# Sigmoid attention and a mixed-block product: unmixed weight blocks kept at their own scale, adds on GpSimd, and another order of seven products

## The chip, the cores and the metric

The kernel runs on one core of one Trainium2 chip. The metric is the device time of one execution in microseconds (us). The core has five engines that run side by side and wait for one another through semaphores: TensorE (PE in the profile, with its weight loads as PEld), VectorE (DVE), ScalarE (ACT), GpSimd (POOL) and SyncE (SP), which here issues nearly all DMAs.

## The reference

The input is 8 batches of 12 heads of attention over 448 positions of 64 values. Its output, 3584 rows of 768, goes through two matrix products with a bent curve between them.

```python
scores = scale * np.matmul(q, k.transpose(0, 1, 3, 2)) - np.log(S)   # q, k, v: 8 x 12 x 448 x 64
attn = 1.0 / (1.0 + np.exp(-scores))
x = np.matmul(attn, v)                       # brought to 3584 x 768
h = x @ w_in                                 # w_in: 768 x 2048
g = np.where(h >= 1, h, np.where(h <= -1, 0, (h + 1) ** 2 / 4))
out = g @ w_out                              # w_out: 2048 x 768
```

## The kernel before

**Numbers in two halves.** Most operands are split into a high and a low f16 half, with a scale that is a power of two, and a product is made of three f16 matmuls (high by high, high by low, low by high). `w_in_sb` holds 16 chunks of w_in, each as two halves of 768 columns; chunks 0 to 7 have the scale `wi.scale[0]`, chunks 8 to 15 `wi.scale[1]`.

**Stages.** Attention is done in pairs of heads, six for a batch; each pair is cut into pieces whose scores (`scores`, L385 to L403), sigmoid (`weigh`, L432 to L444) and product with v (`av`, L476) follow one another. A pair's data is loaded three pairs ahead and split two pairs ahead (`prep_b`, L351 to L366; for pairs from 17 on GpSimd does the splitting, L356 to L358). Pieces of the next batch's attention are spread between the units of the MLP of the batch before. The MLP has `ups` (x by w_in), `bend` (the curve, L713 to L717) and `downs` (g by w_out, L736, with its scaling L742 or L746). `finish_x` scales and splits x (L499 on ScalarE, L500 on VectorE) ahead of the ups of batches 0 and 1.

**Batches 0 and 1 and the mixes.** Batches 0 and 1 use w_in as it is (`up`, L700). While batch 1 is under way, `mix(i)` makes, for each of the eight pairs of chunks f = i and g = i + 8, a set of seven blocks of 384 columns, and sends it to the DRAM tensor `blocks[i]`. Four blocks are mixed, that is sums and differences of the four half chunks a11, a12 (of f) and a21, a22 (of g): the halves are added up to f32 (L610, `mixa`), combined (L614 to L617), scaled and split again (L623 on ScalarE, L624 on VectorE, `mixs`) and sent (L627). Three blocks are plain: both halves of f and the right half of g, multiplied to the common scale of the set (L633, `mixp`) and sent (L636). `mixed["to"][0]` and `["to"][1]` are the factors from the scales of f and g to the common one. `mixa`, `mixs` and `mixp` take turns in the two buffers of the tag `raww`.

**Batches 2 to 7 in blocks.** From batch 2 on, `up_blocks(b, i, j)` makes the ups of a pair of chunks with seven products of half size in place of eight: product j multiplies block `wt` of the set by a block `xt` of x (made by `finish_blocks`, L519 to L526) and adds it up in quarter q of two PSUM tiles of one bank each: quarters 0 and 1 lie in `hold[i, 0]`, quarters 2 and 3 in `hold[i, 2]`. Each product is nine matmuls of 224 columns (L666). ScalarE copies (L678, L684) and VectorE adds (L675) bring the quarters together in hf and hg, which `bend` takes. A matmul with `start=True` begins the sum anew; the others add to it. The three sets in SBUF lie where w_in was; `load_set` (L642) brings in set n + 2 when product 2 of set n is reached, and must wait until the buffer's former set has been used by its last product.

**What sets the order.** The Tile framework makes each engine's instruction stream when the program is built: it goes by priorities (the order in which the code asks for the work, shifted by `tc.high_priority`) and by a model of when each instruction will be ready, and passes over those that aren't. On the chip each engine then runs its stream in that order. The pool `ps_mo` has three PSUM banks, which the tiles `pm`, `ph` and `po` take in turn.

Of the kernel before, what the change touches and what calls it, by code (L numbers as in the profile page):

```python
# [15 lines left out]
F16 = mybir.dt.float16  # L16
BF16 = mybir.dt.bfloat16
I32 = mybir.dt.int32
AF = mybir.ActivationFunctionType
ALU = mybir.AluOpType  # L20
# [3 lines left out]
P = 128  # L24
# [30 lines left out]
QA = 17  # L55
QT = 3
WOP = 6
MIXP = 0
CORN = 10
TP = 1  # L60

# [11 lines left out]
def sigmoid_attention_mlp(ctx: ExitStack, tc: tile.TileContext, first_qvk, qkv, w_in, w_out, out_t):  # L73
    nc = tc.nc
    NFULL, _, _, S = first_qvk.shape
    B = out_t.shape[1] // S
    NFC, _, DM = w_out.shape
# [10 lines left out]
    raw_p = ctx.enter_context(tc.tile_pool(name="raw", bufs=2))  # L88
# [14 lines left out]
    w_in_sb = const.tile([P, NFC + 1, 2, DM], F16, name="w_in_sb")  # L103
# [7 lines left out]
    HN, NB, HC = S // 2, 7, NCC // 2  # L111
# [8 lines left out]
    blocks = drm_p.tile([NFC // 2, P, SET], F16, name="blocks")  # L120

    def scales(m, n, tag, pool=None, square=False, less=0):
# [24 lines left out]
        out=ident, in_=ident, pattern=[[-1, P]], compare_op=ALU.is_equal, fill=0.0, base=0, channel_multiplier=1  # L147
# [438 lines left out]
    mixed = {}  # L586
# [17 lines left out]
    def mix(i):  # L604

        to, ratio, minus = mixed["to"], mixed["ratio"], mixed["minus"]
        f, g, H = i, i + NFC // 2, DM // 2
        a = raw_p.tile([P, 2 * DM], I32, tag="raww", name="mixa").bitcast(F32).rearrange("p (r n) -> p r n", r=2)
        for r, chunk in ((0, f), (1, g)):
            (nc.gpsimd if r < MIXP else nc.vector).tensor_tensor(  # L610
                out=a[:, r], in0=w_in_sb[:, chunk, 0, :], in1=w_in_sb[:, chunk, 1, :], op=ALU.add
            )
        a11, a12, a21, a22 = a[:, 0, :H], a[:, 0, H:], a[:, 1, :H], a[:, 1, H:]
        nc.vector.tensor_tensor(out=a22, in0=a21, in1=a22, op=ALU.add)  # L614
        nc.vector.scalar_tensor_tensor(out=a21, in0=a11, scalar=ratio, in1=a21, op0=ALU.mult, op1=ALU.subtract)
        nc.vector.scalar_tensor_tensor(out=a11, in0=a11, scalar=minus, in1=a22, op0=ALU.mult, op1=ALU.add)
        nc.vector.scalar_tensor_tensor(out=a12, in0=a12, scalar=ratio, in1=a11, op0=ALU.mult, op1=ALU.subtract)  # L617
        st = raw_p.tile([P, 2 * DM], I32, tag="raww", name="mixs").bitcast(F16)
        sv = st.rearrange("p (r t h n) -> p r t h n", r=2, t=2, h=2)
        for r in range(2):  # L620
            src = a[:, r].rearrange("p (t n) -> p t n", t=2)
            hi = sv[:, r, :, 0, :]
            nc.scalar.activation(hi, src, AF.Copy, scale=to[1])  # L623
            nc.vector.scalar_tensor_tensor(  # L624
                out=sv[:, r, :, 1, :], in0=src, scalar=to[1], in1=hi, op0=ALU.mult, op1=ALU.subtract
            )
        nc.sync.dma_start(out=blocks[i][:, 3 * DM :], in_=st)  # L627
        pl = raw_p.tile([P, 2 * DM], I32, tag="raww", name="mixp").bitcast(F16)[:, : 3 * DM]
        pv = pl.rearrange("p (t h n) -> p h t n", t=3, h=2)
        for t0, n, chunk, k in ((0, 2, f, 0), (2, 1, g, 1)):  # L630
            src = w_in_sb[:, chunk].rearrange("p h (t n) -> p h t n", t=2)[:, :, 2 - n :, :]
            for h in range(2):
                nc.vector.tensor_scalar(  # L633
                    out=pv[:, h, t0 : t0 + n, :], in0=src[:, h], scalar1=to[k], scalar2=None, op0=ALU.mult
                )
        nc.sync.dma_start(out=blocks[i][:, : 3 * DM], in_=pl)  # L636

    def load_set(n):

        if n < (B - SB) * NFC // 2:  # L640
            dst = sets[n % 3].rearrange("p t h n -> p (t h n)")
            nc.sync.dma_start(out=dst, in_=blocks[n % (NFC // 2)])  # L642
# [3 lines left out]
        common_scales(b, small("invq", inv_x, 0.25, ALU.mult), small("ihc", inv_x, mixed["inv"], ALU.mult))  # L646


    PRODUCTS = (0, 0, 0), (3, 4, 1), (5, 5, 2), (6, 3, 3), (1, 1, 0), (2, 6, 2), (4, 2, 3)

    def up_blocks(b, i, j):

        n = (b - SB) * (NFC // 2) + i
        if j % 2 == 0 and j < 4:
            hold[i, j] = ps_mo.tile([P, 512], F32, tag="mo", name="ph")
        if j == 2 and n:
            load_set(n + 2)
        wt, xt, q = PRODUCTS[j]

        def quarter(q):  # L660
            return hold[i, q // 2 * 2][:, q % 2 * 256 : q % 2 * 256 + HN]

        out, w = quarter(q), sets[n % 3]
        for c in range(HC):
            for wh, xh in ((0, 0), (0, 1), (1, 0)):
                nc.tensor.matmul(  # L666
                    out, w[:, wt, wh, c * P : (c + 1) * P], xc[:, xt, c, xh, :],
                    start=j in (0, 2) and c + wh + xh == 0, stop=c == HC - 1 and wh == 1,
                    skip_group_check=True,
                )  # L670

        hf, hg = (rows[:, (i % 2 * 2 + k) * S : (i % 2 * 2 + k + 1) * S] for k in range(2))
        u2, u3 = (rows[:, 4 * S + i % 2 * S + k * HN : 4 * S + i % 2 * S + (k + 1) * HN] for k in range(2))

        add = lambda out, q, other: nc.vector.tensor_tensor(out=out, in0=quarter(q), in1=other, op=ALU.add)  # L675
        with tc.high_priority(offset=Q_PRIO):
            if j == 1:
                nc.scalar.activation(u2, quarter(0), AF.Copy)  # L678
                add(u2, 1, u2)
            elif j == 3:  # L680
                add(u3, 2, u2)
                add(hg[:, HN:], 3, u3)
            elif j == 4:
                nc.scalar.activation(hf[:, :HN], quarter(0), AF.Copy)  # L684
            elif j == 6:
                add(hg[:, :HN], 2, u2)
                add(hf[:, HN:], 3, u2)
        if j == 6:
            bend(b, i + NFC // 2, hg)
            bend(b, i, hf)  # L690
# [16 lines left out]
    def bend(b, f, h):  # L707

        ihr, hr, rt, ihs, _ = up_sc[b, int(f >= NA)]
        g = tmp_p.tile([P, S], F32, tag="tmp", name="g")  # L710
        hi = ghl[:, f, 0, :]

        nc.scalar.activation(g, h, AF.Relu, bias=hr, scale=ihr)  # L713
        nc.vector.scalar_tensor_tensor(out=g, in0=g, scalar=rt, in1=g, op0=ALU.min, op1=ALU.mult)  # L714
        nc.vector.scalar_tensor_tensor(out=g, in0=h, scalar=ihs, in1=g, op0=ALU.mult, op1=ALU.max)  # L715
        nc.scalar.activation(hi, g, AF.Copy)  # L716
        (nc.gpsimd if f % GPOOL else nc.vector).tensor_tensor(out=ghl[:, f, 1, :], in0=g, in1=hi, op=ALU.subtract)  # L717

    part = drm_p.tile([NCC, P, S], F32, name="part")
# [33 lines left out]
    def ups_blocks(b):  # L753

        n = NFC // 2
        order = [(0, j) for j in range(4)]
        for i in range(n):
            if i + 1 < n:
                order += [(i + 1, 0), (i + 1, 1)]
            order += [(i, 4), (i, 5), (i, 6)]  # L760
            if i + 1 < n:
                order += [(i + 1, 2), (i + 1, 3)]
        return [lambda i=i, j=j: up_blocks(b, i, j) for i, j in order]
# [72 lines left out]
    for u, unit in enumerate(units):  # L836
# [3 lines left out]
        if wi.at < NFC + 1:  # L840
            n = NPIECE - WI_A
# [4 lines left out]
        f, r = divmod(u, NCC // 2)  # L846
# [25 lines left out]
    for b in range(1, B):  # L872
# [10 lines left out]
        with ExitStack() as order:  # L883
            if b >= PM:
                order.enter_context(tc.manual_schedule(engines={mybir.EngineType.PE}))
            for u, unit in enumerate(units):
                while at < min(b + 2, B) * NPIECE and (at - first) < share[min(u + 1, last)] * NPIECE:
                    step(at)
                    at += 1
                if b == 1:  # L890
                    while split_at < min(NFC, NA + (u + 1) * (NFC - NA) // (NA * NCC // 2 - 2)):
                        wo.split(split_at, split_at % WOP == 1)
                        split_at += 1
                    while mixed_at < NFC // 2 and u >= MIX0 + mixed_at * (MIX1 - MIX0) // (NFC // 2):
                        mix(mixed_at)
                        mixed_at += 1
                if b + 1 < B and u == last:
                    begun = start_blocks()
                unit()
                if b + 1 < B and u == last:  # L900
                    inv_x = finish_blocks(*begun)
                    block_scales(b + 1, inv_x)
                if b == 1 and u == last - 2:
                    for n in range(3):
                        load_set(n)
# [39 lines left out]
```

## Time and profile before

| | us |
|---|---|
| median of 3 runs | 1183.58 (1179.28 to 1185.38) |
| the profiled execution | 1182.99 |
| its span, first to last instruction | 1181.3 |
| TensorE busy | 1146.3 |
| VectorE busy | 824.9 |
| ScalarE busy | 697.1 |
| GpSimd busy | 321.6 |
| mean granted TensorE clock | 0.987 |

How to read the profile: a row of a group names the line, the engine, the operation, what is written and read, shapes and count; after the bar stand busy us and the mean length of one instruction in ns, and after the second bar the engine's idle time just before them with what ended it. A row of the timeline has start and length in us, and in brackets the engine's idle time before it and what ended it. A row of a stretch has its bounds, its length, then busy us and instructions of PE, PEld, DVE, ACT and POOL, the granted clock, the DMA share and GB/s. Matmuls are pipelined, so the mean length of one is longer than its share of the busy time.

### The profile page before, as it was taken

What the parts mean: (1) busy time and instruction counts of PE and PEld (TensorE: products, weight loads), DVE (VectorE), ACT (ScalarE), POOL (GpSimd) and SP (SyncE); (2) the same over time, 40 slices, a digit from 0 to 9 for tenths busy, and PEclk for the clock granted to TensorE, in tenths of its full rate; (3) what the DMA queues carried; (4) which work ended last, traced back from release to release, by engine and by line L of the source; (5) the groups of instructions that cost most, each with busy time, mean ns of one, the idle gap of its engine ahead of it and who ended that gap; (6) DMA issues with size and microseconds to landing.
All of it is one profiled execution on the core that took longest, in us unless ns stands there. A gap on an engine that the chain in (4) does not pass through costs nothing.

```text
span 1181.3 us, 20203 instructions
## 1 busy us (share of the span) xinstructions
PE 1146.3 (97%) x7662; PEld 669.0 (57%) x7662; DVE 824.9 (70%) x1760; ACT 697.1 (59%) x1158; POOL 321.6 (27%) x389
## 2 busy tenths in 40 slices
PE   5889999899999999999999999999999999999998
PEld 1224433344445776457755677457764677558954
DVE  4877999898945588467973689466883678736830
ACT  5975885665743587447763577546874486513410
POOL 0004310000332254325354236232534253310000
PEclk8899999899999999999999999999999999999999
DMA  9941544447532366224643165424552146302400
GB/s 361 335 150 61 195 149 132 151 142 244 176 109 64 119 213 212 64 64 150 253 146 100 33 251 193 132 64 141 196 207 68 61 155 223 117 25 98 153 16 32
DMA packets 58113, 170.01 MB, mean 144 GB/s; under 512 B 8608, under 2 KB 39840, under 8 KB 51872
## 3 DMA queue, kind: packets, MB, share of 16 engines
q1 hardware_dynamic: 56288, 159.29, 39.4%
q10 hardware_dynamic: 1728, 9.44, 2.3%
q8 instruction: 60, 0.98, 0.3%
q14 instruction: 37, 0.30, 0.1%
HBM read 126.94 MB, written 23.40 MB: 127 GB/s over the span
## 4 chain that ended last, share of the span: by engine, by line
PE 76%; DVE 9%; DMA 8%; ACT 4%; issue 1%; POOL 1%; SPq 0%; ACTq 0%; DVEq 0%
PE po L736 35%; PE ph L666 23%; PE pav L476 8%; PE psc L394 3%; PE psc L403 3%; DMA blocks<-mixs 2%; PE ph L700 2%; DMA w_out_sb<-w_in 2%; PE psc L389 1%; DMA raw<-qkv 1%; ACT a L432 1%; DVE g L714 1%; DMA w_out_sb<-w_out 1%; DMA w_in_sb<-blocks 1%; DVE mixs L624 1%
## 5 line engine op out<-in xcount | busy, mean ns | idle before, releaser
L736 PE MATMUL po<-ghl,w_out_sb 128*128 128x448 f16 x2304 | 445.7, 353 | 0.9 <-DVE g L715 0.9
L736 PEld LDWEIGHTS <-w_out_sb 128*128 128x128 f16 x2304 | 221.8, 98 | 216.6 <-issue 14.0
L666 PE MATMUL ph<-w_in_sb 128*128 128x224 f16 x3024 | 307.7, 259 | 2.0 <-DMA w_in_sb<-blocks 1.6
L666 PEld LDWEIGHTS <-w_in_sb 128*128 128x128 f16 x3024 | 282.6, 98 | 30.9 <-issue 27.4
L444 DVE SCALAR_TENSOR_TENSOR ahl<-psc,ahl 128x896 f16<-128x896 f32 (+1 forms) x170 | 152.9, 900 | 112.7 <-ACT ahl L443 110.4
L435 ACT ACTIVATE psc<-psc,nls,sqk 128x896 f32<-128x896 f32 (+1 forms) x136 | 129.4, 971 | 114.7 <-PE psc L403 97.2
L356 POOL TENSOR_SCALAR raw<-raw,qkv_s 128x448 f32<-128x448 f32 (+1 forms) x93 | 71.3, 781 | 452.9 <-DVE qkv_i L136 363.0
L443 ACT ACTIVATE ahl<-psc 128x896 f16<-128x896 f32 (+1 forms) x170 | 126.9, 762 | 32.9 <-DVE ahl L444 31.8
L700 PE MATMUL ph<-xhl,w_in_sb 128*128 128x448 f16 x576 | 115.5, 358 | 5.2 <-DVE xhl L500 2.9
L675 DVE TENSOR_TENSOR xhl<-ph,xhl 128x224 f32<-128x224 f32 x240 | 87.7, 382 | 26.2 <-PE ph L666 19.7
L322 ACT ACTIVATE dump<-raw 128x448 f16<-128x448 f32 (+1 forms) x105 | 61.8, 588 | 69.0 <-DMA raw<-qkv 68.0
L476 PE MATMUL pav<-ahl,v 128*64 128x448 f16 x748 | 95.6, 359 | 0.0
L713 ACT ACTIVATE g<-xhl,hr,ihr 128x448 f32<-128x448 f32 x96 | 68.7, 752 | 44.0 <-DVE xhl L675 43.1
L716 ACT ACTIVATE ghl<-g 128x448 f16<-128x448 f32 x128 | 72.7, 573 | 36.7 <-DVE g L715 36.3
L700 PEld LDWEIGHTS <-w_in_sb 128*128 128x128 f16 x576 | 55.9, 99 | 64.0 <-issue 16.4
L717 DVE TENSOR_TENSOR ghl<-g,ghl 128x448 f16<-128x448 f32 x128 | 85.6, 675 | 7.1 <-ACT ghl L716 6.6
L714 DVE SCALAR_TENSOR_TENSOR g<-g,rk 128x448 f32<-128x448 f32 x112 | 81.1, 739 | 10.7 <-ACT g L713 10.5
L746 DVE TENSOR_SCALAR o<-po,od 128x448 f32<-128x448 f32 x48 | 32.5, 679 | 65.8 <-PE po L736 65.6
L358 POOL TENSOR_TENSOR hl<-raw,hl 128x448 f16<-128x448 f32 x62 | 70.0, 1149 | 0.0
L394 PE MATMUL psc<-qk 128*128 128x448 f16 x252 | 66.6, 354 | 0.4 <-issue 0.3
L715 DVE SCALAR_TENSOR_TENSOR g<-xhl,ihs,g 128x448 f32<-128x448 f32 x96 | 65.5, 699 | 0.3
L385 PE MATMUL psc<-ghl 64*128 64x448 f32 (+1 forms) x128 | 37.4, 672 | 21.9 <-ACT a L432 17.1
(156 smaller groups left out, 1150.0 us busy)
## 6 DMA issues: line engine op xcount, KB each, us to landing
w_in_sb<-blocks SPq DMA_DIRECT2D x48, 1344.0 KB, 6.5
raw<-qkv SPq DMA_DIRECT2D x34, 704.0 KB, 4.9
qk<-hl SPq DMA_DIRECT2D x320, 56.0 KB, 2.0
w_out_sb<-w_in SPq DMA_DIRECT2D x16, 768.0 KB, 10.9
out_t<-o SPq DMA_DIRECT2D x48, 224.0 KB, 1.9
blocks<-mixs SPq DMA_DIRECT2D x8, 768.0 KB, 4.3
w_out_sb<-w_out ACTq DMA_DIRECT2D x6, 768.0 KB, 4.3
raww<-w_out ACTq DMA_DIRECT2D x6, 768.0 KB, 5.4
```

Source lines behind the costliest of these rows:

```text
L394: nc.tensor.matmul(out, kq[:, j, 1, w], kq[:, j, 0, :], start=True, stop=False)
L435: nc.scalar.activation(a, a, AF.Sigmoid, bias=nls, scale=sqk)
L443: nc.scalar.activation(hi, x, AF.Copy, scale=ATT)
L444: nc.vector.scalar_tensor_tensor(out=lo, in0=x, scalar=ATT, in1=hi, op0=ALU.mult, op1=ALU.subtract)
L476: nc.tensor.matmul(pav[j * D : (j + 1) * D, :S], *terms[j][t], start=c == 0 and t == 0, stop=mid and t == len(terms[j]) - 1,)
L666: nc.tensor.matmul(out, w[:, wt, wh, c * P : (c + 1) * P], xc[:, xt, c, xh, :], start=j in (0, 2) and c + wh + xh == 0, stop=c == HC - 1 a ...
L675: add = lambda out, q, other: nc.vector.tensor_tensor(out=out, in0=quarter(q), in1=other, op=ALU.add)
L700: nc.tensor.matmul(ph[:, :S], w_in_sb[:, f, wh, c * P : (c + 1) * P], xhl[:, c, xh, :], start=c == 0 and wh + xh == 0, stop=c == NCC - 1 a ...
L714: nc.vector.scalar_tensor_tensor(out=g, in0=g, scalar=rt, in1=g, op0=ALU.min, op1=ALU.mult)
L716: nc.scalar.activation(hi, g, AF.Copy)
L717: (nc.gpsimd if f % GPOOL else nc.vector).tensor_tensor(out=ghl[:, f, 1, :], in0=g, in1=hi, op=ALU.subtract)
L736: nc.tensor.matmul(po[:, :S], w_out_sb[:, f, wh, m * P : (m + 1) * P], ghl[:, f, gh, :], start=f == lo and wh + gh == 0, stop=f == hi - 1 ...
```

## The change

In `mix`, the two adds that bring the halves of a chunk together run on GpSimd in place of VectorE. The three plain blocks are no longer scaled into a buffer: three DMAs per pair send them to `blocks[i]` straight from `w_in_sb`, with the scale of their chunk. So the factors come in later, in `up_blocks`: the copies of quarter 0 (j = 1 and j = 4) take the factor of f, and the product with the plain block of g, which is now the last one, begins quarter 2 anew and is multiplied by the factor of g and added to u3 in one instruction. The product of quarter 3 that was last is now the one before it, and its add follows at j = 5.

```diff
     for r, chunk in ((0, f), (1, g)):
-            (nc.gpsimd if r < MIXP else nc.vector).tensor_tensor(
+            nc.gpsimd.tensor_tensor(
                 out=a[:, r], in0=w_in_sb[:, chunk, 0, :], in1=w_in_sb[:, chunk, 1, :], op=ALU.add
             )
...
         nc.sync.dma_start(out=blocks[i][:, 3 * DM :], in_=st)
-        pl = raw_p.tile([P, 2 * DM], I32, tag="raww", name="mixp").bitcast(F16)[:, : 3 * DM]
-        pv = pl.rearrange("p (t h n) -> p h t n", t=3, h=2)
-        for t0, n, chunk, k in ((0, 2, f, 0), (2, 1, g, 1)):
-            src = w_in_sb[:, chunk].rearrange("p h (t n) -> p h t n", t=2)[:, :, 2 - n :, :]
-            for h in range(2):
-                nc.vector.tensor_scalar(
-                    out=pv[:, h, t0 : t0 + n, :], in0=src[:, h], scalar1=to[k], scalar2=None, op0=ALU.mult
-                )
-        nc.sync.dma_start(out=blocks[i][:, : 3 * DM], in_=pl)
+        for t, chunk, part in ((0, f, 0), (1, f, 1), (2, g, 1)):
+            dst = blocks[i][:, t * DM : (t + 1) * DM].rearrange("p (h n) -> p h n", h=2)
+            nc.sync.dma_start(out=dst, in_=w_in_sb[:, chunk, :, part * H : (part + 1) * H])
...
-    PRODUCTS = (0, 0, 0), (3, 4, 1), (5, 5, 2), (6, 3, 3), (1, 1, 0), (2, 6, 2), (4, 2, 3)
+    PRODUCTS = (0, 0, 0), (3, 4, 1), (5, 5, 2), (6, 3, 3), (1, 1, 0), (4, 2, 3), (2, 6, 2)
...
-                    start=j in (0, 2) and c + wh + xh == 0, stop=c == HC - 1 and wh == 1,
+                    start=j in (0, 2, 6) and c + wh + xh == 0, stop=c == HC - 1 and wh == 1,
...
             if j == 1:
-                nc.scalar.activation(u2, quarter(0), AF.Copy)
+                nc.scalar.activation(u2, quarter(0), AF.Copy, scale=mixed["to"][0])
                 add(u2, 1, u2)
             elif j == 3:
                 add(u3, 2, u2)
                 add(hg[:, HN:], 3, u3)
             elif j == 4:
-                nc.scalar.activation(hf[:, :HN], quarter(0), AF.Copy)
+                nc.scalar.activation(hf[:, :HN], quarter(0), AF.Copy, scale=mixed["to"][0])
+            elif j == 5:
+                add(hf[:, HN:], 3, u2)
             elif j == 6:
-                add(hg[:, :HN], 2, u2)
-                add(hf[:, HN:], 3, u2)
+                nc.vector.scalar_tensor_tensor(
+                    out=hg[:, :HN], in0=quarter(2), scalar=mixed["to"][1], in1=u3, op0=ALU.mult, op1=ALU.add
+                )
```

More of the change, by code (lines that the diff above doesn't have):

```diff
@@ L57 @@
 WOP = 6
-MIXP = 0
 CORN = 10
```

## The prediction

> **What bounds the kernel now.** I read the page first (busy shares), then the busy time of each engine by stretch, then the list of who waited for whom on TensorE, then the timeline around each of TensorE's waits.
>
> ```profile
> span 1181.3 us, 20203 instructions
> PE 1146.3 (97%) x7662; PEld 669.0 (57%) x7662; DVE 824.9 (70%) x1760; ACT 697.1 (59%) x1158; POOL 321.6 (27%) x389
> ```
>
> ```profile
> 206.70:236.30 29.60, 26.55 (x120) 10.70 (x119) 25.91 (x61) 19.13 (x26) 1.72 (x1) 0.88 0.43 151
> ...
> 180.00:325.00 145.00, 138.73 (x728) 63.46 (x727) 132.88 (x270) 91.50 (x143) 19.71 (x20) 0.98 0.51 171
> ...
> 413.50:443.00 29.50, 29.50 (x266) 22.42 (x264) 25.18 (x56) 24.37 (x46) 16.37 (x20) 1.00 0.60 213
> ...
> 360.00:1181.30 821.30, 815.29 (x6036) 532.45 (x6033) 534.08 (x1191) 454.07 (x783) 258.35 (x320) 1.00 0.37 127
> ```
>
> Columns of the second fence: stretch, its length, busy PE, PEld, DVE, ACT, POOL, granted clock, DMA share, GB/s. TensorE is the bound: from 360 us on it idles 6 us in 821. The blocks (batches 2 to 7) run there, so making VectorE's work lighter there buys nothing. The one stretch in which VectorE is nearly full (132.88 of 145) and TensorE misses 6.3 us is 180 to 325, batch 1, where the mixes of w_in are made. There the clock also falls, to 0.88 in one slice.
>
> ```profile
> PE psc L385 <- ACT a L432: 17.1, 8, 4.2
> ...
> PE ph L700 <- DVE xhl L500: 2.9, 1, 2.9
> PE ph L700 <- DVE g L715: 1.9, 1, 1.9
> PE ph L666 <- DMA w_in_sb<-blocks: 1.6, 1, 1.6
> PE po L736 <- DVE g L715: 0.9, 1, 0.9
> ...
> PE psc L389 <- DVE ahl L444: 0.4, 1, 0.4
> PE ph L666 <- DVE xhl L675: 0.4, 1, 0.4
> ```
>
> TensorE's waits: total us, times, longest. L385 is the start of the program, which the change leaves alone. In batch 1 stand 2.9, 1.9, 0.9 and 0.4, together 6.1. In the 48 blocks stand 1.6 for a set of weights and 0.4 for an add.
>
> ```profile
> 214.63 0.96 DVE L610 TENSOR_TENSOR mixa<-w_in_sb 128x768 f32<-128x768 f16 x1 [1.72 <-DMA blocks<-mixs]
> ...
> 215.57 1.01 DVE L265 SCALAR_TENSOR_TENSOR w_out_sb<-w_out_sb,wo_s 128x768 f16<-128x768 f32 x1
> 216.50 0.95 DVE L610 TENSOR_TENSOR mixa<-w_in_sb 128x768 f32<-128x768 f16 x1
> 217.37 0.68 DVE L500 SCALAR_TENSOR_TENSOR xhl<-x,x_s,xhl 128x448 f16<-128x448 f32 x1
> ...
> 218.10 6.11 PE L700 MATMUL ph<-xhl,w_in_sb 128*128 128x448 f16 x18 [2.93 <-DVE xhl L500]
> ...
> 256.19 1.83 DVE L610 TENSOR_TENSOR mixa<-w_in_sb 128x768 f32<-128x768 f16 x2 [1.88 <-DMA blocks<-mixs]
> ```
>
> The longest of them is the mix's doing: VectorE stands 1.72 us at L610 for the DMA that must leave the raww buffer, then does both adds, and L500, for which TensorE waits, comes behind. The wait of 0.9 at 260 us follows the same pair, there 1.88 + 1.83 us.
>
> **The change part by part.**
>
> ```profile
> L666 PE MATMUL ph<-w_in_sb 128*128 128x224 f16 x3024 | 307.7, 259 | 2.0 <-DMA w_in_sb<-blocks 1.6 <-DVE xhl L675 0.4
> L444 DVE SCALAR_TENSOR_TENSOR ahl<-psc,ahl 128x896 f16<-128x896 f32 (+1 forms) x170 | 152.9, 900 | 112.7 <-ACT ahl L443 110.4
> L700 PE MATMUL ph<-xhl,w_in_sb 128*128 128x448 f16 x576 | 115.5, 358 | 5.2 <-DVE xhl L500 2.9 <-DVE g L715 1.9
> L675 DVE TENSOR_TENSOR xhl<-ph,xhl 128x224 f32<-128x224 f32 x240 | 87.7, 382 | 26.2 <-PE ph L666 19.7 <-ACT xhl L678 3.4 <-PE psc L156 2.7
> L485 ACT ACTIVATE x<-pav,sqk 128x448 f32<-128x448 f32 x34 | 21.5, 632 | 6.8 <-PE pav L476 6.8
> L610 DVE TENSOR_TENSOR mixa<-w_in_sb 128x768 f32<-128x768 f16 x16 | 14.7, 953 | 6.1 <-DMA blocks<-mixs 6.1
> L262 POOL TENSOR_TENSOR w_in_sb<-w_in_sb 128x768 f16<-128x768 f32 x8 | 14.6, 1829 | 9.2 <-ACT w_in_sb L261 9.2
> L633 DVE TENSOR_SCALAR mixp<-w_in_sb,mixes 128x768 f16<-128x768 f16 (+1 forms) x32 | 9.8, 362 | 0.0
> L482 ACT ACTIVATE x<-pav 128x448 f32<-128x448 f32 x14 | 7.5, 538 | 1.9 <-PE pav L476 1.9
> ```
>
> ```profile
> L627 SPq DMA_DIRECT2D blocks<-mixs x8: 320/330/453, 189.7 to 319.8; - x8
> ```
>
> *Scalings removed.* 32 instructions of L633, 9.8 us of VectorE in batch 1. With them goes the third buffer of each mix: mixa and mixs now alternate on the two raww buffers, so mixa waits for no DMA and L610's 6.1 us of idle go. Late next is mixs, which waits for the DMA of the mixs before it, a whole mix back (130 / 7 = 18 us, by the first and the last issue of L627).
>
> *Adds moved.* 16 adds leave VectorE: 14.7 us. On GpSimd the nearest row is L262, the same 768 elements: 16 x 1.83 = 29.3 us, beside the 19.71 us it is busy in that stretch. L614 and L615 now wait for GpSimd, and whatever is behind them on VectorE with them. GpSimd holds two adds (3.7 us) ahead of whatever it is given next, such as the split of q, k and v late in the stretch; a pair is prepared two pairs ahead, so I count nothing. If that lead were gone, 3.7 us would be the price, once.
>
> ```profile
> 185.43 1.87 POOL L262 TENSOR_TENSOR w_out_sb<-w_out_sb 128x768 f16<-128x768 f32 x1 [19.90 <-ACT w_out_sb L261]
> ...
> 185.71 2.40 DVE L624 SCALAR_TENSOR_TENSOR mixs<-mixa,mixes,mixs 128x768 f16<-128x768 f32 x1
> ...
> 188.64 1.00 DVE L624 SCALAR_TENSOR_TENSOR mixs<-mixa,mixes,mixs 128x768 f16<-128x768 f32 x1
> ```
>
> *What GpSimd's adds take from VectorE.* The same L624 takes 2.40 us under a GpSimd add and 1.00 alone: 1.40 us lost in a collision. So 16 adds cost VectorE between nothing and 22.4 us; I take half, 11, as part of VectorE's work reads PSUM and may not collide. VectorE is relieved of 9.8 + 14.7 + 6.1 - 11 = 20 us in 145.
> The Trainium skill, SBUF — State Buffer, section Who interferes with whom, says that a VectorE instruction with two SBUF inputs contends with a GpSimd instruction that reads SBUF, and that the one that comes later is blocked for the whole instruction; the pair of rows agrees. By that rule, with every add meeting such an instruction, the loss is the upper end, 22.4, and the sum that of rival two.
>
> *Stalls that go.* 2.93 + 0.86 + 1.88 + 0.42 = 6.1 us (the four rows). Behind the first, 18 matmuls of L700 took 6.11 us where 115.5 / 576 = 0.20 each gives 3.6: 2.5 us lost to the lower clock and to L500's pace. At most 8.6 us. I keep one collision, 1.4, in front of an L500, and half of the other three waits, 1.6. Gain 5.6.
>
> *DMAs.* 24 small ones from w_in_sb replace 8 from mixp: 16 more issues on SP.
>
> ```profile
> w_in_sb<-blocks SPq DMA_DIRECT2D x48, 1344.0 KB, 6.5
> ```
>
> 16 x 0.33 = 5.3 us of SP over 130 (L627); each waits only for w_in's split, made long before. The bytes are the same. The sets are read back at 390 us, so nothing waits; if that cover were gone it would be one landing, 6.5.
>
> *Scale in the copies.* L485 (with a scale from SBUF) against L482 (without): 94 ns. On the copies of L678 and L684, 96 in 48 blocks, 9.0 us of ScalarE in 800, of which TensorE sees nothing as long as adds are as early as now. The last add with a scale (scalar_tensor_tensor) costs between an add of 224 (0.38) and L500's 0.68 for 448; I take 0.38: nothing changes.
>
> *The new order.* Now hf's add reads quarter 3 between products 5 and 6, and product 6 writes quarter 2 of the same bank.
>
> ```profile
> 527.62 3.62 PE L666 MATMUL ph<-w_in_sb 128*128 128x224 f16 x36
> ...
> 529.55 0.36 ACT L678 ACTIVATE xhl<-ph 128x224 f32<-128x224 f32 x1 [0.26 <-PE ph L666]
> ```
>
> The first 18 of these matmuls are products 0 and 1 of a block. L678 reads quarter 0, which product 0 had finished at 528.6, yet idle ScalarE starts at 529.55, when product 1 in the other half of the bank has ended. So accesses to one bank are kept apart, and product 6 will wait for that add. Its price by block, if nothing is put between: 0.38 plus some 0.05 to start, 0.43; if an L444 (0.90) is running, 1.28. Between 0 and 48 x 1.28 = 61 us, then; a gain is excluded, for nobody waits on what gets earlier.
> The Trainium skill, PSUM — Partial Sum Buffer, section PSUM bank collisions raise a hardware error, asks for exactly this guard, by bank and not by address; the trace agrees with the 529.55 above. By it the sum would be that of rival one.
> Cover is there: TensorE's order is fixed at build time by a scheduler that passes over what isn't ready. Two products of the next block and the attention's matmuls are free to go in between: 18 matmuls of L666 are 1.83 us (307.7 / 3024 each), more than 1.28.
>
> ```profile
> 547.50 0.69 DVE L675 TENSOR_TENSOR xhl<-ph,xhl 128x224 f32<-128x224 f32 x2 [0.80 <-PE ph L666]
> ...
> 550.08 1.89 PE L666 MATMUL ph<-w_in_sb 128*128 128x224 f16 x18
> ```
>
> As I read the order, these adds free the bank that the 18 matmuls at 550.08 take: ready at 548.2, issued 1.9 us later with other work between. That is the same kind of turn, TensorE to VectorE and back, and over 48 blocks it cost 0.4 us in all. I take 0.02 a block, 1.0.
> *Sum.* The profiled execution took 1182.99 us: 1182.99 - 8.6 + 3.0 + 1.0 = 1178.4. The median of the runs, 1183.58, stands 0.6 above it, so 1179.0.
>
> **The rivals.**
> *One, slower: product 6 waits in the open.* From 0.12 us a block (5.6 / 48) the gain is eaten; at 0.43 it is 20.6 us, less 5.6: 1198.6. For it: VectorE is 85% full where the blocks meet attention (25.18 of 29.5), so an add can come late. Against it: the 0.4 us above.
> *Two, no gain:* GpSimd's adds take back 22.4 us of VectorE's 30.6, mixes wait for GpSimd, and the waits only move: 1183. For it: 185.71. Against it: two of the three long waits have L610 itself in front.
> *Three, everything goes:* all 8.6 us and no price, 1175.0.
> *Four, late sets:* the load of a set starts when product 6 has left its buffer. In batch 7, without attention, one load already cost 1.6 us; product 6 slides up to 1.83 later, and five loads at 1.6 are 8: 1186.
>
> **How the numbers follow.** Half a per cent, 5.9 us, is about what a measurement of this kernel can tell from no change. Forecast (1176 to 1182) 0.50; three 0.13; two 0.19; one 0.13; four 0.05. Faster than 1177.7: three and 0.22 of the forecast, 0.35. Slower than 1189.5: one and 0.04 of two and four, 0.17. The rest, 0.48, is no change. The range goes from just under three to most of one: 1174 to 1194.
>
> **What would show it.** Right: in 180 to 325 VectorE near 119 busy and GpSimd near 49; no wait of L610 for a DMA; the wait of L700 for L500 under 1.5 us and no slice at 0.88; from 360 us on TensorE's idle time as before. Wrong: many waits of L666 for L675 (rival one), L624 and L500 at 2 us (two), more waits for w_in_sb<-blocks after 1073 us (four).

## The result: 0.56% slower

| | before | after |
|---|---|---|
| median of 6 runs each (us) | 1183.84 (1179.28 to 1186.69) | 1189.51 (1188.96 to 1191.48) |
| profiled execution, span (us) | 1182.99, 1181.3 | 1188.96, 1187.2 |

The ratio is 1.0056, with a 95% interval from 1.0037 to 1.0074. I had forecast 1179.0. In the experiments below, one execution of `last_on_gpsimd` took 4055.59 us, against 1178.91 to 1183.07 for its other ten; it is left out of the figures.

### The profile after

Two lines of the page: the span, and each engine's busy time.

```profile
span 1187.2 us, 20204 instructions
...
PE 1143.2 (96%) x7662; PEld 666.3 (56%) x7662; DVE 820.7 (69%) x1712; ACT 704.4 (59%) x1158; POOL 345.9 (29%) x405
```

VectorE and TensorE are busy for less time than before, and yet the program is longer. By stretch (columns as in the prediction), first the kernel before with one batch of blocks, batch 2, from the first matmul of its blocks to the first of the next batch's:

```profile
390.40:527.60 137.20, 137.20 (x1023) 88.48 (x1021) 94.80 (x213) 86.83 (x152) 54.12 (x68) 1.00 0.42 143
```

And the kernel after: batch 1 with the mixes, everything from 360 us on, and the same batch of blocks.

```profile
180.00:325.00 145.00, 138.63 (x749) 64.70 (x748) 124.13 (x233) 92.85 (x150) 49.33 (x42) 0.99 0.45 147
360.00:1187.00 827.00, 813.06 (x6001) 527.56 (x5999) 536.33 (x1184) 458.19 (x776) 251.32 (x318) 1.00 0.37 125
...
384.00:524.00 140.00, 138.01 (x1022) 88.14 (x1021) 95.61 (x213) 87.47 (x152) 53.42 (x68) 1.00 0.42 140
```

A batch of blocks took 137.2 us, all of it TensorE's. It now takes 140.0, of which 2.0 are idle and 0.8 are more time for the same matmuls. From 360 us on TensorE idles 13.9 us, where it had idled 6.0 before; I had named no change there as a sign of being right. In batch 1 VectorE fell from 132.88 to 124.13, but TensorE is no fuller (138.63 for 138.73).

Where the stages begin (their first matmul in the timeline, in us) shows which stages gained and which lost:

| us | before | after | difference |
|---|---|---|---|
| first up of batch 0 | 87.5 | 83.9 | -3.6 |
| last up of batch 0 | 166.8 | 162.1 | -4.7 |
| blocks of batch 2 | 390.4 | 383.9 | -6.5 |
| blocks of batch 7 | 1072.9 | 1079.5 | +6.6 |
| last matmul | 1177.6 | 1183.5 | +5.9 |

So 4.7 us were gained before the mixes had begun, 1.8 in the stretch of the mixes, and 13.1 lost in five batches of blocks (2 to 6). TensorE's waits in those blocks and, in the last three rows, in batch 1 (total us, times, longest):

```profile
PE psc L393 <- DVE ahl L443: 3.3, 9, 1.0
PE ph L659 <- DVE xhl L668: 2.8, 5, 0.6
PE po L732 <- ACT ghl L712: 2.0, 4, 0.7
PE po L732 <- DVE ghl L713: 0.8, 4, 0.2
...
PE ph L696 <- ACT xhl L498: 3.1, 1, 3.1
PE ph L696 <- DVE g L711: 2.3, 2, 1.5
PE ph L696 <- DVE xhl L499: 0.6, 1, 0.6
```

`ahl` are the halves of the attention weights and `ghl` those of g. The first four are new, bar 0.4 for an add and 0.4 for `ahl`, and small one by one: in batch 2 scores wait 0.58 for VectorE's L443, which still reads the PSUM tile that they write, the blocks 0.56 for an add, and the downs 0.85 for ghl, together the 2.0. The last three add up to 6.0, as much as the 6.1 that were to go. The groups of the blocks:

```profile
L659 PE MATMUL ph<-w_in_sb 128*128 128x224 f16 x3024 | 305.0, 259 | 3.5 <-DVE xhl L668 2.8 <-DMA w_in_sb<-blocks 0.7
L668 DVE TENSOR_TENSOR xhl<-ph,xhl 128x224 f32<-128x224 f32 x192 | 72.2, 383 | 23.9 <-PE ph L659 20.1 <-ACT xhl L671 2.9
...
L609 POOL TENSOR_TENSOR mixa<-w_in_sb 128x768 f32<-128x768 f16 x16 | 29.8, 1883 | 48.7 <-DVE qkv_e L129 16.8 <-DVE mixs L623 13.4 <-DVE q L533 11.2
...
L681 DVE SCALAR_TENSOR_TENSOR xhl<-ph,mixes,xhl 128x224 f32<-128x224 f32 x48 | 21.5, 447 | 30.7 <-PE ph L659 30.2
L671 ACT ACTIVATE xhl<-ph,mixes 128x224 f32<-128x224 f32 x48 | 21.3, 444 | 21.9 <-PE ph L659 21.9
```

The scaled copy takes 444 ns, 92 more than before's 352, and the scaled add 447, 65 more than the plain 382.

### The profile page after: what moved, and what is told of

Read it like the earlier page. It is cut to its first block, busy times and chain, and to the rows that moved or that the text cites. A ratio compares the mean times of both kernels' runs of the same rounds, so it can differ in the third digit from the quotient of the medians.

```text
span 1187.2 us, 20204 instructions
## 1 busy us (share of the span) xinstructions
PE 1143.2 (96%) x7662; PEld 666.3 (56%) x7662; DVE 820.7 (69%) x1712; ACT 704.4 (59%) x1158; POOL 345.9 (29%) x405
## 4 chain that ended last, share of the span: by engine, by line
PE 59%; DVE 8%; DMA 3%; POOL 3%; ACT 3%; issue 2%; SPq 1%; POOLq 0%; DVEq 0%
PE po L732 29%; PE ph L659 16%; PE pav L475 5%; PE psc L393 2%; PE ph L696 2%; DMA raw<-qkv 2%; DVE ahl L443 2%; PE psc L402 2%; DVE ghl L713 1%; PE psc L388 1%; DVE g L711 1%; DVE xhl L668 1%; POOL raw L355 1%; DMA w_in_sb<-blocks 1%; ACT dump L321 1%
## 5 line engine op out<-in xcount | busy, mean ns | idle before, releaser
L443 DVE SCALAR_TENSOR_TENSOR ahl<-psc,ahl 128x896 f16<-128x896 f32 (+1 forms) x170 | 152.4, 899 | 77.0 <-ACT ahl L442 74.2
L321 ACT ACTIVATE dump<-raw 128x448 f16<-128x448 f32 (+1 forms) x105 | 61.7, 588 | 87.6 <-DMA raw<-qkv 86.6
L713 DVE TENSOR_TENSOR ghl<-g,ghl 128x448 f16<-128x448 f32 x128 | 92.2, 725 | 19.0 <-ACT ghl L712 18.4
L475 PE MATMUL pav<-ahl,v 128*64 128x448 f16 x748 | 98.8, 360 | 0.7 <-DMA qk<-hl 0.7
L710 DVE SCALAR_TENSOR_TENSOR g<-g,rk 128x448 f32<-128x448 f32 x112 | 81.5, 745 | 21.1 <-ACT g L709 20.1
L668 DVE TENSOR_TENSOR xhl<-ph,xhl 128x224 f32<-128x224 f32 x192 | 72.2, 383 | 23.9 <-PE ph L659 20.1
L711 DVE SCALAR_TENSOR_TENSOR g<-xhl,ihs,g 128x448 f32<-128x448 f32 x96 | 69.4, 739 | 0.3
L475 PEld LDWEIGHTS <-v 128*64 128x64 f16 x748 | 36.4, 109 | 41.3 <-issue 27.6
```

The costliest lines, as they stand in the source:

```text
L443: nc.vector.scalar_tensor_tensor(out=lo, in0=x, scalar=ATT, in1=hi, op0=ALU.mult, op1=ALU.subtract)
L475: nc.tensor.matmul(pav[j * D : (j + 1) * D, :S], *terms[j][t], start=c == 0 and t == 0, stop=mid and t == len(terms[j]) - 1,)
```

## The experiments

My theories after the result: the order of the products costs time in the blocks (A), or the scaled forms do (B), or the mixes and their DMAs do (C). Ratios are against the kernel before, on the same chip.

**Which product waits.** `after_lines` is the changed kernel with its products on lines of their own.

```diff
+                if j == 4: nc.tensor.matmul(*args, **kw)
+                elif j == 5: nc.tensor.matmul(*args, **kw)
+                elif j == 6: nc.tensor.matmul(*args, **kw)
...
```

> The changed kernel with the matmul call of products 4, 5 and 6 written on lines of their own; the instruction streams are those of the changed kernel. Both theories expect 1189 us. Theory one (the bank wait): from 384 us on a batch takes 140.0 us against 137.2 before because the build puts product 6 behind 19 to 35 other matmuls (2 to 6 us) after product 5; the direct wait of product 6 for the add stays under 1 us a batch, and the loss shows as waits of downs for a late bend and of scores for a late attention operation. Theory two (the scaled forms are slower: 447 against 382 ns for the last add, 444 against 352 ns for the copies): the waits stand right behind L681, L671 or L677.

Its one execution took 1189.43 us. The only product with a wait for an add is L664, product 5:

```profile
PE ph L664 <- DVE xhl L675: 2.6, 5, 0.6
...
PE ph L668 <- DMA w_in_sb<-blocks: 0.4, 1, 0.4
```

Product 6, which by rival one would wait for the bank, waits for nothing on the chip. In TensorE's stream, 19 to 35 other matmuls stand between products 5 and 6 of a block in batch 3; in `add_at_6` (below), where no add stands between the two products, there are none in seven of eight blocks. They are products of the next blocks and, in six of the eight blocks, attention's matmuls (behind the last block downs as well). The build hides the bank's wait by putting other work there.

**The order alone, and the order undone.** `order_alone` is the kernel before with the new order of products and plain forms. `add_at_6` is the changed kernel with hf's add after the last product, as before, so that nothing reads the bank between products 5 and 6.

```diff
 order_alone (on the kernel before)
-    PRODUCTS = ..., (1, 1, 0), (2, 6, 2), (4, 2, 3)
+    PRODUCTS = ..., (1, 1, 0), (4, 2, 3), (2, 6, 2)
+            elif j == 5:
+                add(hf[:, HN:], 3, u2)
             elif j == 6:
                 add(hg[:, :HN], 2, u2)
-                add(hf[:, HN:], 3, u2)
 add_at_6 (on the kernel after)
-            elif j == 5:
-                add(hf[:, HN:], 3, u2)
             elif j == 6:
                 nc.vector.scalar_tensor_tensor(...)
+                add(hf[:, HN:], 3, u2)
```

> The kernel before with only the order of the last two products changed and hf's add at j = 5; plain blocks are still scaled in batch 1, nothing is on GpSimd that was not, and quarter 2 goes on adding. Theory one (bank wait): a batch takes 139 to 141 us in place of 137.2, 1192 to 1199 us in all. Theory two (scaled forms): none is here, 1182 to 1186. Theory three (any new order): 1180 to 1195.

> The changed kernel with hf's add moved from j = 5 to j = 6, behind the last product, so that no engine reads the bank between products 5 and 6. Theory one (bank wait): products 5 and 6 stand together again, a batch takes 137.2 to 137.8 us, and the gain of batch 1 (batch 2 starts 6.5 us earlier than before) is left: 1174 to 1179 us. Theory two (scaled forms): they are all still there, a batch still takes 140: 1188 to 1191. Theory three (any new order of instructions moves a batch by some us, up or down): no fixed value, 1176 to 1190.

`order_alone`: 1190.07, ratio 1.0050 (1.0030 to 1.0071). Its first batch of blocks, and its largest wait from 390 us on:

```profile
389.60:528.40 138.80, 138.30 (x1023) 87.80 (x1021) 99.40 (x213) 86.12 (x152) 53.96 (x68) 1.00 0.42 141
```
```profile
PE psc L394 <- DVE ahl L444: 2.9, 5, 1.1
```

The order alone makes a batch 138.8, a little less than the 139 to 141 of my first theory: 0.5 of waits, and 1.1 more for the same matmuls, with no lower clock. What makes them longer is what they stand beside. Where TensorE goes from one of the shapes 128*128, 64*128 and 128*64 to another after a matmul of 448 columns, the next matmul starts 279 to 310 ns after the last (mostly 285), where it is 189 within a run of 448 columns, so some 0.1 us goes at each change. Before has 64 such changes in a batch, `order_alone` 75, the changed kernel 70. Eleven at 0.1 are the 1.1. Over the kernels of this text, in batches without a lower clock, TensorE's busy time goes with the count: 136.2 to 136.5 us with 59 changes, 136.6 to 136.7 with 61, 137.2 to 137.6 with 64, 137.8 with 69, 138.1 with 70 and 138.3 with 75. The Trainium skill, TensorEngine Tiling (Array Packing), section Tiling Modes, says that a change of mode drains TensorE; the starts agree, and put a number to it.

`add_at_6`: 1187.92, ratio 1.0027 (1.0011 to 1.0043). That does not bring the gain back, so A is not the whole. It has only 61 changes, yet its batch takes 140.9. Its largest wait, stretches (one batch, then the time around the turn from ups to downs) and timeline there:

```profile
PE po L738 <- ACT ghl L718: 8.8, 4, 2.5
```
```profile
385.20:526.10 140.90, 138.44 (x1024) 89.00 (x1023) 97.27 (x213) 88.19 (x152) 54.09 (x68) 0.99 0.41 139
...
605.00:612.00 7.00, 4.86 (x27) 2.41 (x26) 1.71 (x4) 5.12 (x11) 0.00 (x0) 1.00 0.50 208
612.00:617.00 5.00, 5.00 (x19) 2.04 (x17) 3.79 (x11) 1.13 (x3) 0.91 (x2) 0.66 0.00 0
```
```profile
606.85 0.58 ACT L321 ACTIVATE dump<-raw 128x448 f16<-128x448 f32 x1 [3.46 <-DMA raw<-qkv]
...
603.24 6.04 PE L738 MATMUL po<-ghl,w_out_sb 128*128 128x448 f16 x31
...
611.41 2.10 PE L738 MATMUL po<-ghl,w_out_sb 128*128 128x448 f16 x7 [2.14 <-ACT ghl L718]
```

In four batches TensorE comes to the last pair's downs before their ghl. ScalarE makes that copy behind L321, which waits for the next pair's raw data. After the 2.14 us the clock is at 0.66 for 5 us, which is another 1.7: together 3.8 in this batch. So it goes in three of the four batches. In the fourth the wait is as long (2.16 us), but the clock stays up behind it, for a reason that no run shows, and the batch takes 138.8:

```profile
892.40:897.40 5.00, 5.00 (x29) 2.23 (x30) 4.00 (x11) 2.62 (x4) 0.34 (x1) 1.00 0.00 0
```

**Is it the scaled forms?** `unscaled_forms` is `add_at_6` with plain copies and a plain last add. `scaled_copies_only` and `scaled_add_only` have one of the two. The factors that are missing in these three are left out of the product, so their outputs are not the reference's; the number of instructions is the same.

```diff
 unscaled_forms (on add_at_6)
-                nc.scalar.activation(u2, quarter(0), AF.Copy, scale=mixed["to"][0])
+                nc.scalar.activation(u2, quarter(0), AF.Copy)
...
-                nc.scalar.activation(hf[:, :HN], quarter(0), AF.Copy, scale=mixed["to"][0])
+                nc.scalar.activation(hf[:, :HN], quarter(0), AF.Copy)
...
-                nc.vector.scalar_tensor_tensor(...)
+                add(hg[:, :HN], 2, u3)
 scaled_copies_only: the last of these three; scaled_add_only: the first two
```

> The kernel of add_at_6 with the two copies of quarter 0 without a scale and the last add as a plain add of u3; the factors of f and g are left out of the blocks, so its output is not the reference's. Theory A: the turn from ups to downs may still be hit; if the dump still comes first, a batch takes 139 to 141 us and the time is 1185 to 1190. Theory B (the 92 ns of each scaled copy and 65 ns of the scaled add, 12 us of ScalarE and VectorE in all, are what makes the chain late): a batch is back at 137.2 and the time is 1172 to 1177.

> add_at_6 with its last add plain: only the two copies of quarter 0 carry the factor of f; the factor of g is left out. Theory one (either scaled form changes the stream that the scheduler builds, and the turn from ups to downs opens again): batches 2 to 6 take 139 to 141 us each as in add_at_6, with a wait of L738's successor for ghl of 1 us or more in batch 3; time 1183 to 1188. Theory two (the copies' 90 ns each are hidden, the add does it): batches near 137.2, time 1175 to 1179.

> add_at_6 with its two copies plain: only the last add carries the factor of g; the factor of f is left out. Theory one (either scaled form changes the stream): batches 2 to 6 take 139 to 141 us, time 1183 to 1188. Theory two (the add, 447 ns for 382 at the end of the block's chain, does it): batches 139 to 141 here, and near 137.2 in scaled_copies_only. Theory three (the copies do it): batches near 137.2 here, time 1175 to 1179, and 139 to 141 in scaled_copies_only.

| | median us | ratio | a batch of blocks, us | changes of shape |
|---|---|---|---|---|
| add_at_6 (both forms scaled) | 1187.92 | 1.0027 (1.0011 to 1.0043) | 140.9 to 138.8 | 61 |
| unscaled_forms | 1176.93 | 0.9965 (0.9953 to 0.9978) | 137.1 to 137.5 | 64 |
| scaled_copies_only | 1175.95 | 0.9936 (0.9913 to 0.9960) | 136.2 to 137.0 | 59 |
| scaled_add_only | 1177.77 | 0.9949 (0.9929 to 0.9969) | 136.6 | 61 |

(Batches 2 to 5.) Without the scaled forms the loss is gone; with either one of them it is gone too. So neither 92 ns on a copy nor 65 ns on an add is the price, and B in its plain form falls, as do the theories that I wrote for the last two. Of these four kernels only the one with both has the bad turn. `scaled_copies_only` at the same place, one batch and the timeline of the turn:

```profile
385.10:521.30 136.20, 136.20 (x1024) 88.51 (x1023) 94.42 (x213) 88.26 (x152) 53.83 (x68) 1.00 0.43 144
```
```profile
598.24 9.48 PE L736 MATMUL po<-ghl,w_out_sb 128*128 128x448 f16 x48
607.56 1.12 PE L393 MATMUL psc<-qk 128*128 128x448 f16 x4
...
610.17 3.01 PE L736 MATMUL po<-ghl,w_out_sb 128*128 128x448 f16 x15
```

Here 48 downs that are ready come in one run, and the next downs come at 610.17 without a wait. In `add_at_6` a run of 31 stands there, and after it TensorE is idle. The matmuls are the same; their order in the stream is another.

**Would another engine close the turn?** In `last_on_gpsimd`, which is `add_at_6` but for this, the high copy for the last pair is made by GpSimd, so that it is not behind L321. `after_last_on_gpsimd` does the same on the changed kernel.

```diff
+        if b >= SB and f % (NFC // 2) == NFC // 2 - 1:
+            nc.gpsimd.tensor_copy(out=hi, in_=g)
+        else:
             nc.scalar.activation(hi, g, AF.Copy)
```

> The kernel of add_at_6, and in batches 2 to 7 the high half of g of the last pair of chunks (7 and 15) is copied by GpSimd in place of ScalarE. Theory A (add_at_6 lost its gain because at the turn from ups to downs the copies of the last pair stand on ScalarE behind a dump that waits for the DMA raw<-qkv): the wait of downs for ScalarE, 2.1 us a batch, and the half clock after it go, a batch takes 137 to 138 us in place of 140.5, and the time is 1173 to 1178. Theory B (the scaled forms make a batch slower wherever they stand): a batch still takes 140, 1186 to 1190.

> The changed kernel, hf's add at j = 5 as it is, with the last pair's high half copied by GpSimd as in last_on_gpsimd. Theory A: the waits of downs for ghl (0.6 to 1.6 us a batch) go, what the order of products costs (1.6 us a batch in order_alone) stays: a batch takes 138.5 to 139.3, 1182 to 1187 us. If the order is the whole loss of the changed kernel, a batch still takes 140 and the time is 1188 to 1190.

```profile
PE po L741 <- DVE ghl L722: 5.9, 4, 2.0
```

`last_on_gpsimd` (the row above): 1180.91, ratio 0.9990 (0.9981 to 1.0000), between my two theories. Four waits at the same place are left, now for the low half on VectorE; only the low clock after them is gone, and a batch takes 138 us. So L321 in front of the copy is a part of it and not all. `after_last_on_gpsimd`: 1186.84, ratio 1.0049 (1.0028 to 1.0071), batches of 139; it has 69 changes of shape, five over before, and 1.46 us of waits in batch 3, and 137.2 + 0.5 + 1.46 is the 139.2 that this batch takes.

**The mixes.** `gpsimd_adds` is the kernel before with the two adds on GpSimd. `last_on_gpsimd_adds_back` is `last_on_gpsimd` with the adds on VectorE.

```diff
 gpsimd_adds
-MIXP = 0
+MIXP = 2
 last_on_gpsimd_adds_back
-            nc.gpsimd.tensor_tensor(
+            nc.vector.tensor_tensor(
```

> The kernel before with only the two adds of each mix on GpSimd; the scaled plain blocks, their buffer and the old order of products stay. If the adds off VectorE bring batch 1's gain, batch 2 starts 3 to 6 us earlier and the time is 1177 to 1181. If collisions on the port of GpSimd and VectorE take it back, batch 2 starts at 390 as before and the time is 1182 to 1186. A batch in blocks takes 137.2 us either way.

> The kernel of last_on_gpsimd with the adds of the mixes back on VectorE. gpsimd_adds started batch 2 no earlier than before (392.3 against 390.4 us). If the adds on GpSimd are a loss by themselves (collisions), batch 2 starts 1 to 3 us earlier than in last_on_gpsimd and the time is 1171 to 1176; if they are part of batch 1's gain, batch 2 starts 2 to 5 us later and the time is 1176 to 1181. A batch in blocks is as in last_on_gpsimd.

`gpsimd_adds`: 1187.19, ratio 1.0025 (1.0011 to 1.0039), above both of my ranges. Its batch 1 and its longest wait there:

```profile
180.00:325.00 145.00, 136.94 (x714) 62.23 (x713) 128.99 (x253) 89.61 (x141) 45.35 (x34) 0.99 0.51 168
```
```profile
PE psc L389 <- POOL v L358: 3.6, 1, 3.6
```

Of the 14.7 us of adds that left VectorE, 12.8 (14 of the 16 adds) had stood in this stretch, and its busy time there fell by 3.9 only: most came back in longer instructions, as in the six L500, 6.5 us for 3.8. And GpSimd's split of v, which follows two of the adds, comes late by 3.6. `last_on_gpsimd_adds_back`: 1181.34, ratio 0.9993 (0.9981 to 1.0006), within the error of `last_on_gpsimd`, though batch 2 starts 3.5 us later in its profile (388.3 for 384.8). The adds on GpSimd earn nothing that the times show.

**A version without the cost.** `scale_in_x` keeps the new mix, and takes the blocks' order, copies and adds from the kernel before. The factors go into x, where `finish_blocks` scales it anyway: blocks 0 and 1 of x meet only f's plain blocks, block 6 only g's. `scale_in_x_vector_adds` has the adds of the mix on VectorE too.

```diff
+        s0, s1 = mixes[:, 6:7], mixes[:, 7:8]
+        for k, o in ((0, s0), (1, s1)):
+            nc.vector.tensor_scalar(out=o, in0=s, scalar1=mixed["to"][k], scalar2=None, op0=ALU.mult)
...
-            nc.scalar.activation(hi, src, AF.Copy, scale=s)
+            st = s0 if t < 2 else s1 if t == 6 else s
+            nc.scalar.activation(hi, src, AF.Copy, scale=st)
...
```

> The mix of the changed kernel (adds on GpSimd, plain blocks sent straight at their own scale), the products' order, plain copies and plain adds of the kernel before; the factors of the plain blocks go into x where finish_blocks splits it, so that blocks 0 and 1 of x carry the factor of f and block 6 that of g, at no instruction per pair of chunks. Theory one (the +2.8 us a batch are the price of the new order and of the scaled forms): batches 2 to 6 return to 137.1 to 137.6 us each, the copies to about 352 ns, the adds to 382; batch 2 starts at 384 to 386 us; the time is 1175 to 1178, ratio 0.993 to 0.997. Theory two (the loss comes from the direct DMAs, from sets that are read back differently): batches stay near 139 to 140 and the time at 1186 to 1190. Theory three (the split of x, now with three factors, puts a new wait between batches): periods 137.2 and one wait of TensorE for xc of 1 us or more at each start of a batch, time 1180 to 1184.

> As scale_in_x, but the two adds of each mix on VectorE as before. Theory one (GpSimd's adds earn what they were meant to in batch 1): batch 2 starts 2 to 4 us later than in scale_in_x and the time is 1178 to 1181. Theory two (the adds on GpSimd are worth nothing, the direct DMAs alone start batch 2 earlier): batch 2 starts within 1 us of scale_in_x, the time within 1.5 us of it. Theory three (GpSimd's adds cost what they take from VectorE, as with the scaled blocks of before): batch 2 starts earlier and the time is 1172 to 1175.

`scale_in_x`: 1179.99 against 1184.89, ratio 0.9955 (0.9939 to 0.9971). `scale_in_x_vector_adds`: 1180.01, ratio 0.9958 (0.9943 to 0.9974). The first is 2 us above my first theory's range. Both are faster than the kernel before, which the changed kernel is not. The batch of blocks of the first, and batch 1 of the second:

```profile
385.10:522.80 137.70, 137.37 (x1023) 88.44 (x1021) 94.43 (x215) 86.75 (x152) 53.78 (x68) 1.00 0.43 143
```
```profile
180.00:325.00 145.00, 138.96 (x744) 64.66 (x742) 127.21 (x248) 93.12 (x149) 23.56 (x27) 0.99 0.45 148
```

A batch takes 137.2 to 138.7 with the direct DMAs in place, so C falls: from 0.9955 to the changed kernel's 1.0056 is 1.0%, 12 us, the size of the 13.1 that the table of starts lays on the blocks. The adds on GpSimd again earn nothing.

## Why the prediction was wrong, step by step

The time fell inside my range, 1174 to 1194, but on the other side of the kernel before, and that it fell inside is partly luck: 4.7 us of gain came from the start, for which I had no reason, and without them the median would be some 1194.

**The new order (forecast 1.0, the step that failed).** I asked what product 6's wait would cost and found that cover would hide it. It did: product 6 never waits. But cover was priced at nothing. What goes in between moves attention's matmuls, of other shapes, to other places: in `order_alone` TensorE changes shape eleven times more in a batch, 1.1 us, and some scores come before VectorE (L444) has read the PSUM tile that they write, 0.5 us. That is 1.6 by five batches, 8 us, and all six batches of blocks of the changed kernel lost 12.4 (13.1, less 0.7 in the last). The chance that I gave to a loss by the order stood on rival one, a wait in the open, which does not occur.

**The scale in the copies (forecast nothing).** Right for each form alone, as the two kernels with one of them show, and wrong for both together: `add_at_6` takes 140.4 to 140.9 in batches 2 to 4 against 136.6 in `scaled_add_only`, with the same 61 changes; 2.14 of wait and 1.7 of clock are 3.8 of the 3.8 to 4.3, and in batch 5, where the clock stayed up, the 2.16 of wait are the whole difference from 136.6 to 138.8. My condition, that TensorE sees nothing as long as adds are as early as now, held for the durations and missed that the build plans with them. The losses by order and by forms do not add up in the changed kernel: its batch is 2.8 longer, 2.0 of it idle.

**Stalls that go (forecast 5.6; TensorE waits as long as before).** The stalls moved, as in rival two, though not at its price: GpSimd's adds took some 11 us from VectorE (below) and not 22.4. The 1.8 that the stretch of the mixes gained are TensorE's busy time, at a granted clock of 0.99 for 0.98; no slice is at 0.88, the lowest at 0.94. At the longest wait, the kernel after (engine's rows, start and length):

```profile
205.25 4.59 POOL L609 TENSOR_TENSOR mixa<-w_in_sb 128x768 f32<-128x768 f16 x2 [1.14 <-DVE mixs L623]
...
209.87 0.56 DVE L613 TENSOR_TENSOR mixa<-mixa 128x384 f32<-128x384 f32 x1 [1.47 <-POOL mixa L609]
...
212.17 0.94 ACT L622 ACTIVATE mixs<-mixa,mixes 128x768 f16<-128x768 f32 x1 [2.37 <-DMA blocks<-mixs]
213.01 3.45 ACT L498 ACTIVATE xhl<-x,x_s 128x448 f16<-128x448 f32 x6
...
213.71 0.73 PE L696 MATMUL ph<-xhl,w_in_sb 128*128 128x448 f16 x3 [3.12 <-ACT xhl L498]
```

L609 waits for no DMA any more, as I had said; I had named mixs as late next and given it 18 us of lead. Two mixes here stand 10 us apart (their L622 at 202.32 and 212.17), and the DMA in between left at 205.13. So ScalarE now waits 2.37 for the buffer, with x's split behind it, where VectorE had waited 1.72. The other two waits are collisions:

```profile
225.04 1.99 DVE L613 TENSOR_TENSOR mixa<-mixa 128x384 f32<-128x384 f32 x1
...
231.12 10.48 PE L696 MATMUL ph<-xhl,w_in_sb 128*128 128x448 f16 x54 [1.53 <-DVE g L711]
...
238.10 2.06 DVE L710 SCALAR_TENSOR_TENSOR g<-g,rk 128x448 f32<-128x448 f32 x1
240.08 1.59 DVE L131 TENSOR_SCALAR qkv_s<-qkv_e 128x3 int32<-128x3 int32 x1
...
242.38 2.81 PE L696 MATMUL ph<-xhl,w_in_sb 128*128 128x448 f16 x14 [0.78 <-DVE g L711]
```

GpSimd does its adds from 221.06 to 225.01, the split of w_out (L261) right behind them to 226.62, and the next two adds from 237.71 to 241.65. L613, L710 and L131 take 0.55, 0.67 and 0.15 elsewhere. L613 meets L261, the other two meet the adds, and VectorE goes from them without a pause to the L711 that TensorE waits for.

**What came out as forecast.** GpSimd's adds: 29.8 us for 29.3. What they take from VectorE: I took 11 of 14.7 as lost, and with and without them VectorE is busy for 162.4 and 166.0 us from 165 to 384 us in the two `scale_in_x` kernels, so 14.7 less 3.6, 11.1, were lost. The 3.7 that a late split would cost if GpSimd's lead were gone: 3.6 in `gpsimd_adds`. The DMAs and the sets: TensorE has no wait of 1 us for either in the changed kernel. Not as forecast: VectorE's busy time in batch 1, which should have been near 119, was 124.1. The stretch holds 37 fewer instructions of VectorE, where 46 that the change takes out had stood in it (14 adds, 32 scalings), so other work, seven instructions of `bend` for one, now falls into it: the program is ahead by some 5 us there.

**What I had not counted: the start.** 4.7 us came before any of the edited code ran. In the kernel before, two rows (ScalarE, TensorE) at 70 us:

```profile
69.61 0.89 ACT L222 ACTIVATE w_out_sb<-w_out_sb 128x768 f32<-128x768 f32 x1 [2.67 <-DMA w_out_sb<-w_out]
...
72.27 0.98 PE L385 MATMUL psc<-ghl 64*64 64x448 f32 x4 [3.59 <-ACT a L432]
```

And after, where the same wait for w_out comes behind the sigmoid that TensorE needs:

```profile
67.62 0.99 ACT L431 ACTIVATE a<-psc,nls 128x896 f32<-128x896 f32 x1
...
70.94 0.90 ACT L221 ACTIVATE w_out_sb<-w_out_sb 128x768 f32<-128x768 f32 x1 [1.90 <-DMA w_out_sb<-w_out]
```

The scheduler laid the whole program out anew. In every kernel with direct DMAs ScalarE has this second order here, and in the three without the first. All but one of the former start their ups at 83.9 to 84.9, the three at 86.2 to 87.5. The one is `last_on_gpsimd_adds_back`, which starts at 87.0: there ScalarE waits 0.99 us for w_out before this place, where the others wait 0.48 at most, and its profiled execution, 1184.24 us, is the longest of its eleven. So the new order at the start comes with the direct DMAs, and the start also varies from one execution to the next. Why the direct DMAs change it was not tested.

**What stays open.** Why the scheduler keeps fewer downs for the turn when both forms are scaled, and more with either, was not found: durations in its model, its priorities and the order in which it meets instructions act together, and only the resulting streams were compared.

## What to carry to other kernels

When a program is scheduled at build time, an edit is priced twice: by its own instructions, and by the stream that is built around it. A dependency that never waits on the chip can still cost, because other work has been moved into its place; count the changes of matmul shape and look at the stage's length per batch, not at the waits alone. And where a factor can go into a scaling that is done anyway, here x's, it costs two tiny instructions a batch and leaves the number of changes of shape in the long stage as it was (64).

## What the runs showed of the hardware

A change of matmul shape on TensorE costs some 0.1 us (279 to 310 ns from start to start for 189 at 448 columns, 189 for 96 at 224), 64 times a batch here. A one-input VectorE instruction of three int32 elements was held up until a GpSimd add had ended (1.59 us for 0.15), which I had expected of instructions with two SBUF inputs alone. The Trainium skill, SBUF — State Buffer, section Who interferes with whom, lists tensor_scalar among the forms that can take the shared ports; the row agrees. And a wait of 2.14 us on TensorE was followed by 5 us at a granted clock of 0.66, so it cost 3.8; so it was behind waits of 2.46 and 2.09 us in the same execution, but behind one of 2.16 us the clock stayed at 1.00.
